# Layer 1's output projections in seven block products between the feed-forward halves

## The chip, the cores and the metric

The kernel runs on one core of a Trainium2 chip. A core has TensorE (PE: matmuls, with the loads of their stationary operand shown apart as PEld), VectorE (DVE), ScalarE (ACT), GpSimd (POOL) and SyncE (SP), each with an instruction queue of its own, and 16 engines for transfers (DMA). Matmuls read SBUF and write PSUM[...]; all other data lie in SBUF or in DRAM. The metric is the device time of one execution in microseconds; the median of several is taken.

## The reference

Two layers, each an attention block and a gated feed-forward block, on 2048 tokens of 1024 features. Both layers use the same weights.

```python
x = x + _A_ref(_layernorm(x), wqkv, wo)
x = x + _B_ref(_layernorm(x), w1, w3, w2)     # twice over
# _A_ref: qkv = x @ wqkv; 32 heads of 32; each token attends to 8 tokens, 2 apart, itself and back;
#         softmax over the 8; o = weighted sum of v; return o @ wo          (wo: 1024 x 1024)
# _B_ref: h = silu(x @ w1) * (x @ w3); return h @ w2                        (3584 wide)
```

The change concerns `o @ wo` of the second layer, which the kernel calls layer 1.

## The kernel before

Tokens go in chunks of 512 (`CH`), four to a layer. A unit is one chunk of one layer; `units` has eight, 0 to 3 of layer 0 and 4 to 7 of layer 1. Unit u runs the feed-forward block of its chunk (`b_stage`, L1276); while it does, the attention of a later chunk goes on in the background, and after it the query, key and value products of unit u + 3 are made (`q_part`, L837), for u from 1 to 4.

*The feed-forward block.* From unit 2 on (`TU`) it is computed by Strassen's scheme in Winograd's form: a product of two matrices is cut into 2 x 2 blocks and made in seven block products, P1 to P7, in place of eight, with sums of blocks made before and after. `products` (L1143) does one of the two parts into which the 3584 hidden features are split, 2048 and 1536 (`fsplits`; called halves below). `pipeline` (L1052) makes the hidden features in groups of four tiles of w1 or w3; `second` (L1226) then multiplies by w2's half, with `W(name, j)` (L1179) for one block product and one of two tiles of 128 tokens. Bank A holds P1, is copied to bank B by ScalarE, and both go on: P2 is added to B, P6 and then P7 and P4 to A, P5 and P3 in D. The copies of A and D that VectorE adds (`s5`, `su`) are ScalarE's. So P2 or P6 waits for the copy after P1, P7 for the copy after P6, and P3 and P4 for VectorE's sums. `output` adds a finished bank to the residual `x_sb`.

*The sums of the weights.* The block sums of w1, w3 and w2 are made in units 0 and 1 (`weight_sums`, `sums_of_w2`): ScalarE scales four blocks into fp16, VectorE makes three differences and a sum, GpSimd's queue stores the seven blocks to DRAM (`t_d`, `t2_d`), and later they are loaded as any weight. The scale is a power of two from the sum of squares (`weight_size`, `total_scale` at L995). For w2 and w1/w3 there are two such buffers; `stored[a]` is the time at which the planner takes a buffer's last store to have landed, 7.0 us after the last difference.

*The attention.* `score_steps` (L583) and `value_steps` (L664) yield VectorE instructions for halves of 256 tokens: products of q and k with sums over each head's lanes in a tree (into `psm`, L593), a matmul that gathers the heads, a softmax, a copy of the weights to all lanes by GpSimd's queue (`At`), products with v and the second tree (into `oT`, in two buffers).

*The output projection.* `o_tile` (L772) does 128 tokens: eight matmuls into each of two 512-column banks, each added to `x_sb` by VectorE. For both layers, it is called from `between` (L814), which runs after each feed-forward group and takes a tile whose `oT` is ready. When a chunk's four tiles are done, its layer norm is queued.

*What sets the order.* The order is written by a planner inside the kernel, when it is built: each engine has a planned time (`now`), each background step a cost and a time at which it is ready. `background` (L135) puts VectorE steps ahead of the next fixed one where they fit; `act_background` (L363) does so for ScalarE's lists, up to `gate` (2.2 us) ahead of TensorE; `finish_sums` and `force` empty a list at once. `load_weight` (L715) requests the weight tiles in the order of the list `seq` on SP's queue, into six buffers, one as each is released.

Of the kernel before, what the change touches and what calls it, by code (L numbers as in the profile page):

```python
# [17 lines left out]
def kernel(  # L18
# [13 lines left out]
    nc = tc.nc  # L32
# [178 lines left out]
    NG = NF // FG  # L211
    ones = const.tile([P, P], FP32, name="ones")
# [8 lines left out]
    peak = const.tile([P, 3], FP32, name="peak")  # L221
    hsum = const.tile([P, HTN // 2, HT], FP16, name="hsum")
    h16 = hT[:].bitcast(FP16)
    t2_d = [dram.tile([P, 7, (b - a) // 2, 512], FP16, name=f"t2_d{i}") for i, (a, b) in enumerate(fsplits)]
    t_d = [[dram.tile([P, 14, KT // 2, P], FP16, name=f"t_d{m}_{g}") for g in range(NG)] for m in range(2)]
    qkv_d = [[dram.tile([P, KT, S], BF16, name=f"qkv_d{l}_{i}") for i in range(3)] for l in range(2)]
# [74 lines left out]
    adds, acts, makes, reads, parts, sizes = [], [], [], [], [], []  # L301
# [61 lines left out]
    def act_background():  # L363
        for queue in (acts, sizes, parts, reads):
            while True:
                s = head(queue)
                if s is None or max(now["act"], s[1]) + s[0] > now["pe"] + gate[0]:
                    break
                take_act(queue)
# [213 lines left out]
    def score_steps():  # L583

        V = nc.vector
        for g, (l, h) in enumerate(halves):
# [6 lines left out]
            psm = wk.tile([P, W, 2, TCH], BF16, name="psm")  # L593
# [6 lines left out]
            parts_ = 2 if l == 0 else 1  # L600
# [6 lines left out]
            def gather_heads(t, parts_=parts_):  # L607
                at["L"] = L = side_tile([P, W, BLK], FP32, name="L", tag="sd")
                for i in range(parts_):
                    for a in range(4):  # L610
                        nc.tensor.matmul(L[32 * a:32 * (a + 1), :, :], lhsT=gather[:],  # L611
                                         rhs=psm[:, :, i, a * BLK:(a + 1) * BLK], start=i == 0, stop=i == parts_ - 1,
                                         skip_group_check=True)
                at["t"] = pe(1.5 * parts_, t) + 0.2
# [38 lines left out]
            yield 0.56, 0.0, lambda: V.reciprocal(rs[:], sm_[:])  # L653
            yield 0.68, 0.0, lambda: V.tensor_tensor(An[:], E[:], rs[:].unsqueeze(1).to_broadcast([P, W, BLK]),
# [9 lines left out]
    def value_steps():  # L664

        V = nc.vector
        for g, (l, h) in enumerate(halves):
            while (l, h) not in At_at or (g >= 2 and o_todo.get(halves[g - 2], 1)):
                yield "blocked"
            load_v(l, h)  # L670
            while (l, h) not in vs:
                yield "blocked"
                load_v(l, h)
            At = Ats[l, h]
            vT, ready = vs[l, h]
            oT = wk.tile([P, KT, TCH], BF16, name="oT", bufs=2)
            oTs[l, h] = oT

            def mul_v(t, tm):
                base = vT[:, t, HALO:HALO + TCH]  # L680
                win = bass.AP(vT.tensor, base.offset, [list(base.ap[0]), [-DIL, W], [BLK, 4], [1, BLK]])
                V.tensor_tensor(tm.rearrange("p w (a e) -> p w a e", a=4), At[:].rearrange("p a w e -> p w a e"), win, op=ALU.mult)  # L682

            yield 0.0, max(ready + 2.0, At_at[l, h]), lambda: None
            yield from tree(KT, tree_bufs[1], mul_v, lambda t: oT[:, t, :], False)
            oT_at[l, h] = now["dve"]
            o_todo[l, h] = 2
            av_done.add((l, h))
            if g + 1 < len(halves):
                load_v(*halves[g + 1])  # L690
# [5 lines left out]
    for u in range(len(units)):  # L696
        for f0, f1 in fsplits:
# [9 lines left out]
            if u >= TU:  # L707
                seq += [("t2", fsplits.index((f0, f1)), b, nq) for b in range(7)]
            else:
                seq += [("w2", g0, nq, hh) for hh in range(2) for g0 in (f0, f0 + nq)]  # L710
# [4 lines left out]
    def load_weight(pieces=1):  # L715
# [11 lines left out]
        elif kind == "t2":  # L727
            w = wp.tile([P, 8, 512], FP16, name="t2", tag="w")
            nc.sync.dma_start(w[:, 0:rest[0], :], t2_d[i][:, n])
            at = dma(128 * rest[0], now["pe"])  # L730
        elif kind in ("early", "late"):
# [105 lines left out]
    def q_part(l, c, which, ws, then=()):  # L837
# [8 lines left out]
        for t0 in range(0, KT, SG):  # L846
# [19 lines left out]
            if l == 0:  # L866
                stored[:] = landed, landed
# [65 lines left out]
    pending, stored, made, held = [0] * 2, [0.0] * 2, set(), []  # L933
# [36 lines left out]
    def measure2(i, n, at):  # L970

        w = hT[:, 0:n, :]
        for a, b in ((0, n // 2), (n // 2, n)):
            def square():
                nc.scalar.activation(junk[:, 0:(b - a) * 512], w[:, a:b, :].rearrange("p k c -> p (k c)"),
                                     ACTF.Square, accum_out=size2[:, len(measured):len(measured) + 1])
                measured.append(i)
                if len(measured) == 16:
                    total_scale(size2, up2, down2, got2)
# [15 lines left out]
    def total_scale(sizes_, up, down, got):  # L995
# [3 lines left out]
        def scale_item(ps, r):  # L999
            def emit():  # L1000
                opened[0] -= 1
                nc.vector.tensor_reduce(total[:], ps[:], op=ALU.add, axis=AX.X)
                scale_of(total[:], up[:], down[:])
# [3 lines left out]
        def add_up(t):  # L1007
            ps = side_tile([P, n], FP32, name="size", tag="sd")
            opened[0] += 1
            nc.tensor.matmul(ps[:], lhsT=ones[:], rhs=sizes_[:], start=True, stop=True)  # L1010
# [5 lines left out]
    got2 = {}  # L1016

    def sums_of_w2(i, f, ws, loaded):

        while "at" not in got2 or all(pending):  # L1020
            yield "blocked"
# [30 lines left out]
    def pipeline(key, groups, consume, done, last, fill=None):  # L1052
# [68 lines left out]
        for i in range(n + 1):  # L1121
# [19 lines left out]
            done(i)  # L1141

    def products(u, f0, f1, hold):  # L1143
# [118 lines left out]
        def done(i):  # L1262
            if i and groups[i - 1]["m"] == 1:
                h_pieces(groups[i - 1]["f"] + FG)
            if i < len(groups):
                between(hold)
            q = u + 3
# [8 lines left out]
    def b_stage(u, hold):  # L1276
# [5 lines left out]
        for (f0, f1) in fsplits:  # L1282
            lastsplit = (f1 == fsplits[-1][1])
            if u >= TU:
                products(u, f0, f1, hold)
                continue
# [106 lines left out]
    for u, (l, c) in enumerate(units):  # L1393
        if u + 1 < len(units):
            l2, c2 = units[u + 1]
            o_queue += [(l2, c2 * TPC + j) for j in range(TPC)]
# [3 lines left out]
        if with_q:  # L1400
            for which in range(3):
                if which == 2:
                    between(False, True)
                q_part(*units[q], which, [weight("qkv"), weight("qkv")])
# [31 lines left out]
```

## Time and profile before

| | |
|---|---|
| median of 3 runs | 1531.34 us (1530.53 to 1531.69) |
| the profiled execution | 1530.2 us, its span 1528.5 us |
| TensorE busy | 1519.7 us, 9634 matmuls |
| VectorE busy | 1202.3 us |
| ScalarE busy | 884.7 us |
| output projections of both layers | 512 matmuls, 115.7 us |
| transfers | 439.56 MB, mean 288 GB/s |

Busy time is the time in which an engine has an instruction of the kernel; two that overlap count once. A row of the groups gives source line, engine, operation, what it writes and reads with shapes, the count, then busy time, the mean of one in ns, and after the bar the engine's idle time just before such instructions with what ended it. In the order of time a row begins with its start in us from the span's start and its length. By the order of time, unit 2's groups begin at 554.96 us, unit 3's at 740.93, unit 4's at 925.85, unit 5's at 1111.72, unit 6's at 1255.22 and unit 7's at 1396.92.

### The profile page before, as it was taken

The page shows a single profiled execution, that of the slowest core. Times are in us where ns is not written, and L with a number is a line of the kernel's source. Part 1 is how long each engine was busy: PE and PEld are TensorE (multiplying, and loading weights), DVE is VectorE, ACT ScalarE, POOL GpSimd, SP SyncE. Part 2 cuts the span into 40 slices and gives each one's busy share as a digit, 9 for nine tenths or more (in the row PEclk, how much of TensorE's full clock was granted, in tenths as well). Part 3 has the DMA queues.
Part 4 walks back from the last instruction along what each step waited for, and adds up shares of the span by engine and source line. Part 5 has one row for each costly group of instructions (what it writes and reads, how often), then busy time and mean ns, then how long its engine had stood idle before and what let it go on. Part 6 is the DMA issues. An engine that isn't in the chain of part 4 may idle for free.

```text
span 1528.5 us, 25134 instructions
## 1 busy us (share of the span) xinstructions
PE 1519.7 (99%) x9634; PEld 989.3 (65%) x9634; DVE 1202.3 (79%) x2126; ACT 884.7 (58%) x1388; POOL 160.0 (10%) x308
## 2 busy tenths in 40 slices
PE   9999999999999999999999999999999999999999
PEld 7666644444444577575786767766677768686865
DVE  4788998889889898979898959798678977535445
ACT  4785476567665357455465564755557446554643
POOL 1210102121211101002001020100111001000000
PEclk9999999999999999999999999999999999999999
DMA  9777969898997888979879888898969887878885
GB/s 336 192 224 215 260 218 334 279 300 283 309 307 257 278 317 293 350 271 294 264 268 356 323 259 282 271 335 304 322 224 331 337 315 266 306 273 336 317 293 204
DMA packets 261432, 439.56 MB, mean 288 GB/s; under 512 B 73856, under 2 KB 201088, under 8 KB 245056
## 3 DMA queue, kind: packets, MB, share of 16 engines
q1 hardware_dynamic: 248464, 390.90, 77.1%
q0 software_dynamic: 12704, 46.93, 8.6%
q8 instruction: 75, 1.23, 0.3%
q14 instruction: 45, 0.37, 0.1%
q10 hardware_dynamic: 144, 0.13, 0.0%
HBM read 345.90 MB, written 67.90 MB: 271 GB/s over the span
## 4 chain that ended last, share of the span: by engine, by line
PE 94%; ACT 3%; DVE 2%; issue 1%; DMA 0%; SPq 0%; ACTq 0%; DVEq 0%
PE st L1069 31%; PE ps L853 21%; PE w L1188 15%; PE po L788 7%; PE pg L1302 6%; PE acc L1333 6%; PE pu L1311 6%; PE pq L444 1%; ACT sg L1250 1%; PE L L611 0%; ACT L639 0%; DMA wqkv<-in_A_wqkv_dram 0%; DVE hT L1159 0%; DVE tree L597 0%; ACT L1250 0%
## 5 line engine op out<-in xcount | busy, mean ns | idle before, releaser
L853 PE MATMUL ps<-xnT,wqkv 128*128 128x512 f16 (+1 forms) x1472 | 320.5, 379 | 0.0
L1069 PEld LDWEIGHTS <-early 128*128 128x128 f16 x2688 | 262.6, 98 | 40.5 <-issue 3.5
L853 PEld LDWEIGHTS <-wqkv 128*128 128x128 bf16 x1472 | 210.7, 144 | 108.0 <-issue 2.2
L1188 PE MATMUL w<-t,hT 128*128 128x512 f16 x1008 | 225.9, 379 | 1.2 <-ACT big L1208 1.1
L1069 PEld LDWEIGHTS <-late 128*128 128x128 f16 x2016 | 197.2, 98 | 28.9 <-issue 1.1
L597 DVE TENSOR_TENSOR tree<-qT,kT 128x2048 bf16<-128x2048 bf16 x128 | 156.2, 1220 | 30.3 <-DMA kT<-qkv_d 14.5
L510 DVE TENSOR_TENSOR tree<-tree 128x1024 bf16<-128x1024 bf16 x256 | 174.8, 684 | 1.0
L1069 PE MATMUL st<-xnT,late 128*128 128x256 f16 x1344 | 174.2, 273 | 0.4 <-DVE big L1106 0.2
L1069 PE MATMUL st<-big,early 128*128 128x256 f16 x1344 | 172.2, 273 | 1.5 <-ACT st L1081 1.4
L1188 PEld LDWEIGHTS <-hT 128*128 128x128 f16 x1008 | 98.3, 98 | 113.7 <-issue 2.4
L1069 PE MATMUL st<-xnT,early 128*128 128x256 f16 x1344 | 165.8, 273 | 0.0
L682 DVE TENSOR_TENSOR tree<-At,vT 128x2048 bf16<-128x2048 bf16 x128 | 156.0, 1218 | 9.3 <-DMA At<-E 8.0
L1081 ACT COPY st<-st 128x512 f32<-128x512 f32 x84 | 48.3, 575 | 125.9 <-PE st L1069 125.2
L788 PE MATMUL po<-wo,oT 128*128 128x512 bf16 x512 | 115.7, 379 | 0.0
L1311 PE MATMUL pu<-xnT,w3t 128*128 128x512 f16 x448 | 105.8, 379 | 0.0
L1302 PE MATMUL pg<-xnT,w1t 128*128 128x512 f16 x448 | 105.8, 379 | 0.0
L857 ACT CAST hT<-ps 128x512 bf16<-128x512 f32 x96 | 55.6, 585 | 86.4 <-PE ps L853 83.0
L1333 PE MATMUL acc<-w2t,hT 128*128 128x512 bf16 x448 | 98.3, 379 | 0.0
L1094 DVE TENSOR_TENSOR st<-st,big 128x512 f32<-128x512 f32 x84 | 58.3, 695 | 45.4 <-ACT big L1090 45.2
L1250 ACT ACTIVATE sg<-st,down_scale 128x512 bf16<-128x512 f32 x126 | 86.7, 688 | 11.9 <-PE st L1069 11.6
L1069 PE MATMUL st<-big,late 128*128 128x256 f16 x672 | 87.1, 273 | 0.0
L788 PEld LDWEIGHTS <-oT 128*128 128x128 bf16 x512 | 50.1, 98 | 55.7
(167 smaller groups left out, 1920.3 us busy)
## 6 DMA issues: line engine op xcount, KB each, us to landing
early<-t_d SPq DMA_DIRECT2D x84, 1024.0 KB, 6.7
late<-t_d SPq DMA_DIRECT2D x84, 768.0 KB, 6.4
t<-t_d SPq DMA_DIRECT2D x42, 1024.0 KB, 7.6
t<-t_d SPq DMA_DIRECT2D x42, 768.0 KB, 5.2
wqkv<-in_A_wqkv_dram SPq DMA_DIRECT2D x28, 1024.0 KB, 7.5
w1t<-in_B_w_dram SPq DMA_DIRECT2D x14, 1024.0 KB, 7.8
w3t<-in_B_w_dram SPq DMA_DIRECT2D x14, 1024.0 KB, 11.3
t_d<-big POOLq DMA_DIRECT2D x28, 512.0 KB, 5.5
```

The costliest lines, as they stand in the source:

```text
L510: nc.vector.tensor_tensor(b, b, buf[:, 4:8, :], op=ALU.add)
L597: V.tensor_tensor(pr, qT[:], kT[:, :, k0:k0 + TCH], op=ALU.mult)
L682: V.tensor_tensor(tm.rearrange("p w (a e) -> p w a e", a=4), At[:].rearrange("p a w e -> p w a e"), win, op=ALU.mult)
L788: nc.tensor.matmul(ps[:], lhsT=oT[:, t, j * P:(j + 1) * P], rhs=wo[:, t, hh * 512:(hh + 1) * 512], start=(t == 0), stop=(t == KT - 1))
L853: nc.tensor.matmul(ps[:], lhsT=ws[kk // KH][:, kk % KH, t::KT], rhs=xnT[:, kk, :], start=(kk == 0), stop=(kk == KT - 1))
L1069: nc.tensor.matmul(out[:, a, :], lhsT=w[:, a, blk, k, :], rhs=rhs[:, k, :], start=start and a == 0 and k == 0, stop=k == KQ - 1, skip_grou ...
L1094: nc.vector.tensor_tensor(G["D"][:], G["D"][:], su, op=ALU.add)
L1188: nc.tensor.matmul(out[:], lhsT=lhs[:, k, j * P:(j + 1) * P], rhs=w[:, k, :], start=start and k == 0, stop=k == nq - 1, skip_group_check=True)
L1250: nc.scalar.activation(sg[:], src, ACTF.Silu, scale=inv)
L1302: nc.tensor.matmul(pg[:], lhsT=w1t[:, kk, fi * P:(fi + 1) * P], rhs=xnT[:, kk, :], start=(kk == 0), stop=(kk == KT - 1))
L1311: nc.tensor.matmul(pu[:], lhsT=w3t[:, kk, fi * P:(fi + 1) * P], rhs=xnT[:, kk, :], start=(kk == 0), stop=(kk == KT - 1))
L1333: nc.tensor.matmul(acc[:], lhsT=hT[:, f, j * P:(j + 1) * P], rhs=tiles[hh][f // nq][:, f % nq, :], start=(f == 0), stop=(f == f1 - f0 - 1))
```

## The change

Layer 1's output projections are made by the same scheme of seven products, as a stage of its own for a whole chunk (`o_products`), after the first half of units 3 to 6. Layer 0's keep `o_tile`. A chunk's two halves of 256 tokens are the rows of blocks, the two halves of wo's 1024 input features the other cut of the left side, and two column halves of 512 that of wo.

For that wo needs its block sums. Sums of squares of wo and of wqkv's value part, in 16 ScalarE instructions, give two powers of two. In unit 2 the sums are made in eight small blocks: four scaled copies on ScalarE, four VectorE instructions and one store by GpSimd's queue each, in one buffer, `spare`. It lies in the half of the score buffer (`psms`, now a fixed tile of the size of `psm`) that only layer 0's scores use. In unit 3, SP's queue loads four of the seven blocks over wo (`wo16`); the other three come for each chunk as two weight tiles ("to"). Layer 1's `oT` is fp16, and its softmax denominators take one of the scales; the outputs are scaled on their way into `x_sb`.

```diff
+    psms = const.tile([P, 2 * W * TCH], BF16, name="psms")
+    spare = psms[:, W * TCH:W * TCH + 7 * TCH].bitcast(FP16).rearrange("p (b c) -> p b c", b=7)
+    wo16 = wo[:].rearrange("p k d -> p (k d)").bitcast(FP16).rearrange("p (b f c) -> p b f c", b=4, f=KT // 2)
...
-        for queue in (acts, sizes, parts, reads):
+        for queue in (acts, sizes, parts, reads, lazy):
...
+            if l == 1:
+                while "at" not in got_a[2]:
+                    yield "blocked"
+                yield 0.12, got_a[2]["at"], lambda: V.tensor_scalar(rs[:], rs[:], up_a[:, 1:2], None, op0=ALU.mult)
...
+                if f0 == 0 and u + 1 < len(units) and units[u + 1][0] == 1:
+                    seq += [("to", 4, 2), ("to", 6, 1)]
...
+        elif kind == "to":
+            w = wp.tile([P, 8, 512], FP16, name="to", tag="w")
+            nc.sync.dma_start(w[:, 0:4 * n, :], to_d[:, i:i + n].rearrange("p b f c -> p (b f) c"))
...
+    def sizes_of(m, w, i0, at):
+        for k in range(w.shape[1]):
+            yield 1.10, at, lambda: nc.scalar.activation(junk[:, 0:D], w[:, k, :], ACTF.Square,
+                                                         accum_out=size_a[:, m, i0 + k:i0 + k + 1])
+        if i0 + w.shape[1] == KT:
+            total_scale(size_a[:, m, :], up_a[:, m:m + 1], down_a[:, m:m + 1], got_a[m])
...
+    def sums_of_wo(at):
+        KQ = KT // 2
+        while (0, NCH * R - 1) not in At_at:
+            yield "blocked"
+        for f, q in ((f, q) for f in range(KQ) for q in range(2)):
+            while pending[2]:
+                yield "blocked"
+            pending[2] += 1
+            for j, (fh, hh) in ((0, (0, 0)), (2, (0, 1)), (1, (1, 0)), (5, (1, 1))):
+                c0 = hh * 512 + q * TCH
+                yield 0.37, max(at, stored[2]), lambda: nc.scalar.activation(
+                    spare[:, j], wo[:, KQ * fh + f, c0:c0 + TCH], ACTF.Copy, scale=up_a[:, 0:1])
+            makes.append([sums_of_wo_block(f, q, now["act"] + 0.1), None])
+        made.add("wo")
+
+    def sums_of_wo_block(f, q, r):
+        for out, x, y in ((4, 5, 2), (2, 2, 0), (3, 4, 0), (6, 1, 3)):
+            yield 0.28, r, lambda: nc.vector.tensor_tensor(
+                spare[:, out], spare[:, x], spare[:, y], op=ALU.add if (x, y) == (4, 0) else ALU.subtract)
+        pending[2] -= 1
+        nc.gpsimd.dma_start(to_d[:, :, f, q * TCH:(q + 1) * TCH], spare)
+        stored[2] = now["dve"] + 7.0
...
+    def o_products(c, hold):
...
+        def h_sum(name, out, x, y, op, r):
+            background(r)
+            nc.vector.tensor_tensor(out, x, y, op=op)
+            at[name] = dve(0.61, r) + 0.1
...
+        def run(name, j, out, start, r=0.0):
+            for k in range(KQ):
+                nc.tensor.matmul(out[:], lhsT=left[name][:, k, j * P:(j + 1) * P], rhs=right[name][:, k, :],
+                                 start=start and k == 0, stop=k == KQ - 1, skip_group_check=True)
+            return pe(KQ, max(r, at.get(name, 0.0)))
...
+        for j in range(2):
+            g = G[j]
+            g["A"] = bank("oA")
+            g["1"] = r = run("P1", j, g["A"], True)
+            g["B"] = bank("oB")
+            nc.scalar.copy(g["B"][:], g["A"][:])
+            g["tB"] = act(0.5, r)
...
+        for j in range(2):
+            g = G[j]
+            r = run("P6", j, g["A"], False, g["tB"])
+            nc.scalar.copy(su[j], g["A"][:])
+            g["tU"] = t = act(0.5, r)
+            background(t + 0.8)
+            nc.vector.tensor_tensor(g["D"][:], g["D"][:], su[j], op=ALU.add)
+            g["tD"] = dve(0.68, max(t, g["t5"])) + 0.1
+        w = weight("to")
+        right["P7"], right["P3"] = w[:, 0:KQ], w[:, KQ:KT]
+        for j in range(2):
+            g = G[j]
+            r = run("P7", j, g["A"], False, g["tU"])
+            background(r + 0.8)
+            nc.vector.tensor_tensor(s22[j], g["A"][:], s5[j], op=ALU.add)
+            g["tC"] = dve(0.68, r) + 0.1
+            output(2 + j, 1, s22[j], g["tC"])
...
+            if (u, f0, i) == (2, 0, 2):
+                finish_sums(lambda: "at" in got_a[0] and "at" in got_a[1])
+                scale_o()
+                reads.append([sums_of_wo(now["act"]), None])
+            if (u, f0, i) == (3, 0, 5):
+                finish_sums(lambda: "wo" in made)
+                force(makes, lambda: not pending[2])
+                nc.sync.dma_start(wo16, to_d[:, 0:4])
+                dma(2048)
...
                 products(u, f0, f1, hold)
+                if f0 == 0 and u + 1 < len(units) and units[u + 1][0] == 1:
+                    o_products(units[u + 1][1], hold)
...
-            o_queue += [(l2, c2 * TPC + j) for j in range(TPC)]
+            if l2 == 0:
+                o_queue += [(l2, c2 * TPC + j) for j in range(TPC)]
...
-                q_part(*units[q], which, [weight("qkv"), weight("qkv")])
+                ws = [weight("qkv"), weight("qkv")]
+                if u == 1 and which == 0:
+                    lazy.append([sizes_of(0, wo, 0, 0.0), None])
+                if u == 1 and which == 2:
+                    lazy.extend([sizes_of(1, ws[i], KH * i, w_at[used[0] - 2 + i]), None] for i in range(2))
+                q_part(*units[q], which, ws)
+                while which == 2 and head(lazy) is not None:
+                    take_act(lazy)
                 release(2)
```

The stage runs P1, P2, P5, P6, P7, P3 and P4 in that order, each for two tiles of 128 tokens, with bank A, B and D and the copies as in `second`, but with a second buffer for the copy of A (`su`).

## The prediction

> **What bounds the kernel now.** I read the page first, then TensorE's waits, then busy time in stretches of layer 1, and last the order of time at the places where the change puts work.
>
> ```profile
> PE 1519.7 (99%) x9634; PEld 989.3 (65%) x9634; DVE 1202.3 (79%) x2126; ACT 884.7 (58%) x1388; POOL 160.0 (10%) x308
> PEclk9999999999999999999999999999999999999999
> ...
> PE 94%; ACT 3%; DVE 2%; issue 1%; DMA 0%; SPq 0%; ACTq 0%; DVEq 0%
> ...
> L788 PE MATMUL po<-wo,oT 128*128 128x512 bf16 x512 | 115.7, 379 | 0.0
> ```
>
> The clock is full throughout and the chain that ended last is 94% matmuls: time falls where matmuls are removed and nothing makes TensorE wait. The last line is the work that the change touches: 512 output-projection matmuls, half of them layer 1's, with no idle time before any. They start 0.216 us apart (sixteen start between 744.43 and 747.88 us); 379 ns is the latency of one.
>
> Busy time by stretch: unit 2 (555 to 741 us), two second halves in unit 3 and 4 that hold feed-forward groups without an output projection in them, and the first half of unit 4, which has four. Columns are length, then busy us of PE, PEld, DVE, ACT, POOL, then clock, DMA share and GB/s.
>
> ```profile
> 555.00:741.00 186.00, 185.23 (x1254) 129.70 (x1253) 163.87 (x282) 110.90 (x176) 23.22 (x40) 1.00 0.89 303
> 829.00:863.00 34.00, 34.00 (x314) 30.46 (x313) 32.90 (x59) 23.23 (x37) 0.00 (x0) 1.00 0.91 325
> 1015.00:1049.00 34.00, 34.00 (x314) 30.48 (x313) 33.18 (x63) 22.56 (x37) 0.00 (x0) 1.00 0.90 308
> 926.00:988.00 62.00, 61.28 (x497) 47.97 (x495) 49.68 (x87) 38.60 (x63) 3.55 (x10) 1.00 0.76 269
> ```
>
> Two things count. VectorE is 88% busy in unit 2 and 97% in the second halves, so work added to it there is late. And groups run without a gap when no output projection stands between them, so taking the projections out of the first halves costs nothing by itself. TensorE's waits between 741 and 1397 us (units 3 to 6) sum to 2.2 us:
>
> ```profile
> PE st L1069 <- ACT st L1081: 1.0, 2, 0.6
> PE w L1188 <- ACT big L1208: 0.8, 2, 0.5
> ```
>
> All are of one kind: a ScalarE copy of a partial sum is late and the next product on that bank waits for it.
>
> [...]
>
> **The change part by part.**
>
> *Products.* Layer 1 has four chunks of 64 matmuls (4 token tiles x 2 column halves x 8). Seven products of 2 token tiles x 4 matmuls are 56. Saved: 4 x 8 x 0.216 = 6.9 us. The two new sums of squares on TensorE are two passes each, whose starts are 29 and 111 ns apart in the trace: 0.14 us each, 0.3 us.
>
> *The squares.* Sixteen squares of 128x1024 come into unit 1's query/key/value part, one behind each evacuation. A like ACT instruction (L318) lasts 1.06 us and its read of the sum 0.20, overlapping to 1.05 us from start to start; with the evacuation's 0.48 that is 1.53 in the 1.73 us in which TensorE makes one output. It fits, but the order shows that the last square stands behind the last evacuation and ahead of the first copy of unit 2. Before, that place looks so:
>
> ```profile
> 554.96 1.04 PE L1069 MATMUL st<-xnT,early 128*128 128x256 f16 x8
> ...
> 555.21 0.59 ACT L857 CAST hT<-ps 128x512 bf16<-128x512 f32 x1 [1.15 <-PE ps L853]
> ...
> 555.83 1.91 PE L1069 MATMUL st<-big,early 128*128 128x256 f16 x16
> ...
> 556.09 0.57 ACT L1081 COPY st<-st 128x512 f32<-128x512 f32 x1 [0.29 <-PE st L1069]
> ```
>
> The copy at 556.09 must end before P6, eight matmuls into the third line, at 556.70. With the square it starts at 555.21 + 0.48 + 1.05 = 556.74 and ends at 557.32: TensorE loses 0.7 us, once.
>
> *The block sums in unit 2.* Eight blocks of four scaled copies (128x256; half of L927's 0.71 us) and four VectorE differences (0.28 us each by the 128x256 row of L514): 12 us on ScalarE, which has 75 idle in the stretch, and 9 us on VectorE, which has 22. So VectorE goes to 93% and its sums and outputs slip. There is one buffer: the next block's first copy waits on ScalarE's queue for the store to land. The planner reckons with 7.0 us after the last difference. The nearest stores, also of 896 rows:
>
> ```profile
> t_d<-big POOLq DMA_DIRECT2D x14, 896.0 KB, 6.4
> ```
>
> and the copies that wait for such a store behind them already stand idle in the trace of before (the waits of L1026):
>
> ```profile
>   DMA t_d<-big: 34.9, 11
> ```
>
> A block is half as many bytes, so it should land in about 6 us from an issue some 0.5 us after the last difference; some will be later than 7. Behind the waiting copy stand the bank copies that P6 and P7 need, with about 1.6 us to spare (three products of 0.87 us, less 0.4 until the result is seen and a copy of 0.58). Cost: nothing if landings are in time, 1.4 us for each of 7 refills if they come 10 us after the last difference. I take 0.8 for landings and 1.5 for VectorE's slip: 2.3 us. The stores stand on POOL's queue among the attention copies; POOL is busy 23 us of the 186, so I take nothing for that.
>
> *The new stage.* One product of a token tile is 4 x 0.216 = 0.86 us. P1's result must be copied to a second bank before P2: last start 0.65, seen 0.42 later (at the border in unit 3, where P4's output starts 0.20 after the next product does, 828.80 against 828.60), copy 0.58, pick-up 0.05, sum 1.70 against the 1.73 after which P2 comes. P6 to P7 is the same. Both hold by 0.03 us, if nothing stands ahead of the copy on ScalarE; the order shows nothing. VectorE has 4 sums of 1024 (0.61 us from start to start, of L1159), 8 outputs (0.67, L1173) and 4 adds (0.60, L1211): 10.2 us in TensorE's 12.1. But the order puts 8, 5, 8 and 0 attention instructions among them, 3.6, 2.6, 3.6 and 0 us. So in three of the four stages VectorE ends 2 to 3 us late. What is late next: P4 of the second tile waits for its sum (about 0.1 to 0.6 us), and the next half's P5 takes a bank that an output frees with three outputs (2.0 us) behind it, so about when P5 comes. I take 0.3 us a stage, 1.2 in all; bounds 0 and 2 us a stage. Before, the same border (828.60, P5 at 829.47) has no wait.
>
> *Loads.* 1.5 MB for each chunk, 2 MB once on SP's queue in unit 3, and 3.7 MB of stores. The once-load waits for the stores: the order puts the last of them at the start of unit 2's query/key/value part, which takes 41.7 us (699.0 to 740.7), and five groups of 6.1 us follow before the load, so they have landed. At 300 GB/s it delays the weight tiles behind it on SP's queue by 7 us. In a second half of before a tile is asked for about 12 us before its use and lands in 6.7, a cover of 5 us: taken at 0, up to 2 us if that fails. In the new stage no weight is asked for, so the queue catches up.
>
> *Other.* Waits that move in the first halves, +0.5 us. The scaling of a 128x64 row, the two-byte type of oT and the fixed score buffer change no duration that I can see.
>
> Sum: -6.9 + 0.3 + 0.7 + 2.3 + 1.2 + 0.5 = -1.9 us. The profiled execution took 1530.2 us, its span 1528.5; so 1528.3 and 1526.6. The median of the runs is 1.1 above that execution: 1529.4 us.
>
> **The rivals.**
> *All waits are hidden.* The pipelines without projections have none in 34 us, and ScalarE has room. Then only the sums of squares and the late square remain: 1531.3 - 6.9 + 1.0 = 1525.4. Against it: VectorE at 97%.
> *The store decides, slower.* Without its 0.8 us the gain is 2.7. If every block lands 9.6 us after its last difference, ScalarE's queue is held 2.6 us beyond plan, less 1.6 to spare: 1 us for each of 7 refills, 7 in all: 1531.3 - 2.7 + 7 = 1535.6. It turns the sign from 0.4 us a refill, a landing 9.0 us after the last difference. For it: the 34.9 us above, a median of 6.4 and a plan of 7.0. Against: half the bytes.
> *VectorE in the new stage.* If it is 2 us late in each of four stages, 8 in place of 1.2: 1536. Against: three outputs lie behind the one that frees the bank, and the last stage has no attention in it.
> *The change only moves the bound.* 11.7 MB more at a DMA share of 0.9 would take 39 us if all of it stood in the way; the chain has DMA at 0%, so a few late tiles: 1532 to 1534.
>
> **How the numbers follow.** Forecast 0.52, in its own range of 1527.3 to 1531.5; all hidden 0.16; the store 0.12; VectorE 0.10; loads 0.10. 0.2%, about what a measurement of this kernel can tell from no change, is 3.06 us: faster is under 1528.28, slower over 1534.40. Faster: all of the second and a quarter of the first, 0.28. Slower: the store and VectorE in most cases, 0.18. The rest, 0.54, is no difference. The range leaves out a tenth at each end: 1525.2 to 1535.2.
>
> **What would show it.** Layer 1's projections with 224 matmuls at 0.216 us and four stages of 12.1 to 12.7 us; a wait of about 0.7 us on a ScalarE copy at the start of unit 2; unit 2 longer by 2 to 4 us and units 3 to 6 shorter by 5 to 6 together. Wrong if ScalarE's waits for the store exceed some us a refill, if a stage takes over 13.5 us, or if TensorE waits for a weight tile.

## The result, and the profile after

The changed kernel took 1537.41 us, the median of 4 runs (1536.69 to 1539.18), beside 1530.93 us (1530.49 to 1531.69) for the kernel before on the same chip: a ratio of 1.0044, 95% interval 1.0026 to 1.0061. It is 6.5 us slower; a time of 1529.4 us, 1.9 less, was forecast. Two of the changed kernel's four runs, 1538.13 and 1539.18 us, show a mean clock of 0.999, while the other two at 1.000 lie 5.8 us above the kernel before. The profiled execution took 1536.69 us, its span 1535.0.

The page of the changed kernel: its engines, TensorE's clock, and the chain of work that ended last.

```profile
PE 1516.7 (99%) x9606; PEld 986.7 (64%) x9606; DVE 1232.4 (80%) x2210; ACT 924.5 (60%) x1476; POOL 157.5 (10%) x316
...
PEclk9999999999999999999999999999999999999999
...
PE 39%; DVE 11%; ACT 4%; issue 2%; DMA 1%; POOL 0%; ACTq 0%; DVEq 0%; POOLq 0%
```

TensorE has less to do than before (1519.7 us) and the clock is full in this execution, so the time is in waits. The chain can't be set beside that of before, in which TensorE had 94%: its shares add up to 57%, as it is followed back only to 662.4 us, where it comes to a store. In the part that it covers VectorE, ScalarE and a transfer have a share. Such shares are not costs, but they name where to look.

The groups by shape show the work that was exchanged (layer 0's tiles first, then the new stage; after the bar, the idle time before such a matmul):

```profile
L805 PE MATMUL po<-wo,oT 128*128 128x512 bf16 x256 | 57.9, 379 | 0.2 <-DVE x_sb L810 0.2
L1231 PE MATMUL oA<-to,oT 128*128 128x512 f16 x64 | 15.4, 379 | 1.3 <-DVE big L1275 1.3
L1231 PE MATMUL oA<-wo,oT 128*128 128x512 f16 x64 | 15.1, 379 | 0.0
L1231 PE MATMUL oD<-wo,hsum 128*128 128x512 f16 x32 | 7.6, 379 | 0.0
L1231 PE MATMUL oD<-to,oT 128*128 128x512 f16 x32 | 7.6, 379 | 0.0
L1231 PE MATMUL oB<-wo,oT 128*128 128x512 f16 x32 | 7.6, 379 | 0.0
```

256 of layer 1's matmuls have become 224 of the same length: 32 x 0.216 = 6.9 us are gone. The saving is real, and 13 us of other time came.

Busy time by unit, 2 to 5 (the columns as in the prediction):

```profile
555.60:747.60 192.00, 186.37 (x1255) 129.63 (x1253) 170.02 (x317) 122.04 (x211) 24.43 (x44) 1.00 0.92 308
747.60:933.90 186.30, 183.19 (x1240) 128.90 (x1237) 153.56 (x259) 114.03 (x181) 17.02 (x40) 1.00 0.94 310
933.90:1117.30 183.40, 182.92 (x1237) 128.84 (x1236) 155.41 (x266) 111.70 (x179) 14.75 (x36) 1.00 0.95 315
1117.30:1262.40 145.10, 142.09 (x1046) 101.43 (x1045) 135.66 (x234) 84.07 (x136) 8.76 (x18) 1.00 0.90 310
```

Before, these units took 185.9, 184.9, 185.9 and 143.5 us. Unit 2, where the block sums are made, is 6.1 us longer. Unit 4 is 2.5 us shorter, near the 1.7 us of the eight matmuls that each of units 3 to 6 lost; units 3 and 5, which lost as many, are longer. From the start of unit 3 to that of unit 7 it is 655.9 us in place of 656.0. So there are two things to explain: unit 2's 6.1 us, and that units 3 to 6 give back all of what they save. What TensorE waited for:

```profile
PE st L1126 <- ACT big L1147: 3.8, 4, 3.0
PE st L1126 <- ACT sg L1405: 2.3, 2, 1.1
PE st L1126 <- DVE st L1151: 1.4, 1, 1.4
PE oA L1231 <- DVE big L1275: 1.3, 2, 0.7
PE w L1343 <- ACT big L1363: 1.3, 3, 0.7
```

Each line is a waiting matmul, what it waited for, the sum, the count and the longest. One wait of 3.0 us for the copy of A (`su`, L1147) is the largest. In order of time, all engines, it looks so:

```profile
634.10 0.28 DVE L1069 TENSOR_TENSOR psms<-psms 128x256 f16<-128x256 f16 x1
...
634.93 0.96 POOL L1072 DMA_DIRECT2D to_d<-psms  x1 [11.95 <-DVE psms L1069]
...
639.34 0.57 ACT L1138 COPY st<-st 128x512 f32<-128x512 f32 x1 [5.74 <-PE st L1126]
...
640.89 1.91 PE L1126 MATMUL st<-xnT,early 128*128 128x256 f16 x16
...
643.84 0.51 ACT L1061 ACTIVATE psms<-wo,up_a 128x256 f16<-128x256 bf16 x1 [3.92 <-DVE tree L519]
644.25 0.58 ACT L1143 ACTIVATE big<-st 128x512 f32<-128x512 f32 x1
644.73 0.50 ACT L1061 ACTIVATE psms<-wo,up_a 128x256 f16<-128x256 bf16 x1
645.13 0.57 ACT L1147 COPY big<-st 128x512 f32<-128x512 f32 x1
...
645.75 0.49 PE L1126 MATMUL st<-xnT,late 128*128 128x256 f16 x3 [2.95 <-ACT big L1147]
```

And the one store of that stretch, from the view of transfers (KB, us from issue to landing):

```profile
to_d<-psms POOLq DMA_DIRECT2D x1, 448.0 KB, 8.5
```

The block's last difference ends at 634.38, GpSimd issues the store at 634.93, and it lands 8.5 us later at 643.5: 9.1 us after the difference, where the planner wrote 7.0. The next block's first scaled copy (L1061) is at the head of ScalarE's queue from 639.9 on and can't write the one buffer until then; ScalarE stands idle for 3.92 us. (The line names a VectorE instruction, L519, as what ended that. It isn't connected with the copy; the landing is what the copy needs.) Behind it stand the copies of D and A (L1143, L1147), whose products were made by 640.9, and P7 on TensorE, due at 642.6, waits for the second.

To compare whole kernels I add, from unit 2 on, the time by which each matmul starts later after the one before than their usual distance (0.108 us for 256 columns, 0.216 for 512), where that is over 0.15 us and the trace shows a releaser:

| us of lateness on TensorE | before | after |
|---|---|---|
| start of unit 2 (to 612 us) | 0 | 1.4 |
| rest of unit 2 and the border to unit 3 | 1.3 | 5.7 |
| behind an exponential and its tables in unit 3 | 0 | 2.6 |
| the new stages and the product after each | 0 | 1.9 |
| all else | 3.6 | 5.7 |
| sum | 4.9 | 17.3 |

12.4 more, less the 6.9 saved, plus the 0.6 by which unit 2 begins later, is 6.1; the spans differ by 6.5.

### The profile page after: what moved, and what is told of

It reads as the page before. It is cut to its first block, busy times and chain, and to the rows that moved or that the text cites. A ratio compares the mean times of both kernels' runs of the same rounds, so it can differ in the third digit from the quotient of the medians.

```text
span 1535.0 us, 25327 instructions
## 1 busy us (share of the span) xinstructions
PE 1516.7 (99%) x9606; PEld 986.7 (64%) x9606; DVE 1232.4 (80%) x2210; ACT 924.5 (60%) x1476; POOL 157.5 (10%) x316
## 4 chain that ended last, share of the span: by engine, by line
PE 39%; DVE 11%; ACT 4%; issue 2%; DMA 1%; POOL 0%; ACTq 0%; DVEq 0%; POOLq 0%
PE st L1126 20%; PE w L1343 10%; PE ps L870 7%; DVE tree L605 1%; DVE tree L517 1%; ACT sg L1405 1%; DVE x_sb L1328 1%; PE oA L1231 1%; DVE hT L1314 1%; DVE tree L693 1%; DVE hT L1414 1%; DVE tree L519 1%; ACT xn L325 1%; PE oD L1231 0%; DMA to_d<-psms 0%
## 5 line engine op out<-in xcount | busy, mean ns | idle before, releaser
L605 DVE TENSOR_TENSOR tree<-qT,kT 128x2048 bf16<-128x2048 bf16 x128 | 156.2, 1221 | 19.5 <-DMA qT<-qkv_d 14.4
L693 DVE TENSOR_TENSOR tree<-At,vT 128x2048 bf16<-128x2048 bf16 x128 | 156.1, 1220 | 13.6 <-DMA At<-E 12.4
L1151 DVE TENSOR_TENSOR st<-st,big 128x512 f32<-128x512 f32 x84 | 58.5, 696 | 58.8 <-ACT big L1147 58.3
L1405 ACT ACTIVATE sg<-st,down_scale 128x512 bf16<-128x512 f32 x126 | 86.6, 687 | 10.3 <-PE st L1126 9.9
L519 DVE TENSOR_TENSOR tree<-tree 128x512 bf16<-128x512 bf16 x192 | 80.3, 418 | 0.0
L1503 PEld LDWEIGHTS <-hT 128*128 128x128 bf16 x448 | 43.7, 98 | 53.2 <-issue 0.8
## 6 DMA issues: line engine op xcount, KB each, us to landing
w3t<-in_B_w_dram SPq DMA_DIRECT2D x14, 1024.0 KB, 12.1
```

Source lines behind the costliest of these rows:

```text
L519: nc.vector.tensor_tensor(b[:, 0:2, :], b[:, 0:2, :], b[:, 2:4, :], op=ALU.add)
L605: V.tensor_tensor(pr, qT[:], kT[:, :, k0:k0 + TCH], op=ALU.mult)
L1151: nc.vector.tensor_tensor(G["D"][:], G["D"][:], su, op=ALU.add)
L1405: nc.scalar.activation(sg[:], src, ACTF.Silu, scale=inv)
L1503: nc.tensor.matmul(acc[:], lhsT=hT[:, f, j * P:(j + 1) * P], rhs=tiles[hh][f // nq][:, f % nq, :], start=(f == 0), stop=(f == f1 - f0 - 1))
```

## The experiments

Two theories stood against each other at first. *The store*: its landing beyond the plan makes the loss. *Full engines*: VectorE and ScalarE are too full for the block sums and the stage, and the store's wait is only where it shows. "The later plan" is the kernel that is told of sixth.

**The blocks stored from elsewhere.** The sums are made, but the store reads another DRAM tensor.

```diff
-        nc.gpsimd.dma_start(to_d[:, :, f, q * TCH:(q + 1) * TCH], spare)
+        nc.gpsimd.dma_start(to_d[:, :, f, q * TCH:(q + 1) * TCH], t2_d[0][:, :, f, q * TCH:(q + 1) * TCH])
```

> Changed kernel, same order on every engine, but the eight stores of unit 2 take their bytes from another DRAM tensor, so no scaled copy waits for a store to land. Left out: wo's real sums (layer 1's projections use w2's blocks). Theory landing (ScalarE stands at the head of its queue until a store has landed, and a bank copy behind it is late): the 3.1 us wait at 645.7 us and most of those at 671 to 690 go, unit 2 is 3.5 to 4.5 us shorter, time about 1533.3. Theory amount of work (ScalarE's and VectorE's added instructions make unit 2 longer, whatever they wait for): within 0.7 us of the changed kernel, 1537.4.

1535.66 us, ratio 1.0028 (1.0017 to 1.0040). Unit 2 fell to 187.3 us, but the run doesn't tell the theories apart, since the edit moved something else: with no block to wait for, the eight stores were issued from 276.9 to 298.3 us, in unit 0, and near them TensorE lost 2.77 us and then ran at a lower clock, 0.90 from 290 to 306 us (order of time, TensorE):

```profile
298.03 1.89 PE L1481 MATMUL pu<-xnT,w3t 128*128 128x512 f16 x8
302.69 5.30 PE L805 MATMUL po<-wo,oT 128*128 128x512 bf16 x16 [2.77 <-DVE x_sb L810]
```

Sixteen matmuls that take 3.6 us take 5.3. Unit 2 begins 4.3 us later than in the changed kernel; from there to the last matmul's start it takes 968.7 us against 975.6. That is the size of the loss, but a comparison of a part.

**No block sums at all**; the stage loads block sums of w2 in their place, so that the projections have wrong weights.

```diff
...
-                reads.append([sums_of_wo(now["act"]), None])
+                made.add("wo")
...
-                nc.sync.dma_start(wo16, to_d[:, 0:4])
+                nc.sync.dma_start(wo16, t2_d[0][:, 0:4, 0:4])
```

> Changed kernel without the eight blocks of copies, differences and stores; the stage loads w2's block sums in wo's place (left out: wo's sums, so layer 1's projections are of other weights). Theory landing and theory amount of work alike: unit 2 falls to 0.7 to 1.5 us above the kernel before (the late square stays), time 1530.5 to 1532. Theory stage (the loss comes from the new stage and from what it shifts in units 3 to 6): time stays above 1535.

1534.82 us, 1.0027 (1.0018 to 1.0036): a miss, between the two times expected. Unit 2 is 187.3 us and unit 3 184.0, but unit 5 is 148.2. There an exponential fell into a gate group. In order of time, ScalarE and TensorE:

```profile
1222.57 1.28 ACT L646 ACT_TABLE_LOAD   x1
1222.69 1.04 PE L1126 MATMUL st<-xnT,late 128*128 128x256 f16 x8
1223.86 0.60 ACT L646 ACTIVATE E<-L 128x512 bf16<-128x512 f32 x1
1224.47 1.28 ACT L1405 ACT_TABLE_LOAD   x1
1225.77 0.69 ACT L1405 ACTIVATE sg<-st,down_scale 128x512 bf16<-128x512 f32 x1
...
1226.51 1.86 PE L1126 MATMUL st<-big,early 128*128 128x256 f16 x8 [2.79 <-ACT sg L1405]
```

The exponential and the silu need different tables; both loads and the exponential, 3.2 us, stand before a silu that holds a bank. And again the clock is lower afterwards, 0.80 from 1226.6 to 1234.0 us: the eight matmuls of the last line take 1.86 us, those of the second 1.04. The four new stages take 1.6 us more in all than in the changed kernel (12.6, 13.9, 13.1 and 12.1 us). Taking work out moved the plan into other waits.

**The block sums alone**, layer 1's projections as before (`o_tile`); the kernel before with the squares, the scaled copies, the differences and their stores.

> Kernel before with the squares, the scales and the eight blocks of unit 2 of the changed kernel, their result unused; layer 1's projections by single tiles as before. Theory landing or amount of work: about 6 us above the kernel before (0.3 for sums of squares, 0.6 for the late square, 5 for the blocks), 1537. Theory stage: 1 us above, 1532.

1543.90 us, 1.0082 (1.0067 to 1.0097): 13 us for the sums and squares without the stage, twice the 6 that were expected of them. So the loss is there without any stage. What the stage itself is worth can't be read from the 6.5 us between this kernel and the changed one, since the plan is another: TensorE's largest other losses are 1.49 us at 850.23, 1.84 at 1027.27 and 1.36 at 1124.83. The copies wait for the store about as in the changed kernel, where five wait for 8.1 us with the 3.92 above (the waits of L1055, the copy's line here):

```profile
  DMA to_d<-psms: 8.8, 6
```

**No attention in the stage**: its calls of `background` go, so that nothing stands between its sums.

```diff
-            background(r)
             nc.vector.tensor_tensor(out, x, y, op=op)
...
-            background(r + 0.8)
             nc.vector.tensor_tensor(s22[j], g["A"][:], s5[j], op=ALU.add)
```

> Changed kernel in which no attention instruction is put among VectorE's work of the new stage. If VectorE's attention work makes P4 of the second tile late in stages one and three (waits of 0.9 and 0.8 us): both waits go, 1.5 to 1.9 us faster than the changed kernel, 1535.7, unless the attention that is put off is missed later. If they come from VectorE's own chain: no change, 1537.4.

1537.34 us, 1.0035 (1.0022 to 1.0049), by the median level with the changed kernel. But both waits in the stage are gone, and all four stages take 12.1 us. In the profiled execution (1537.83 us, mean clock 0.999) the eight matmuls behind the store's wait in unit 2 take 1.86 us in place of 1.03 (last section), which hides a gain: from the start of unit 3 to the last matmul's it takes 782.5 us, the changed kernel 783.5. So of the 1.5 to 1.9 us expected about 1 came, by one execution of each kernel, and a part went where the attention went (waits of 0.9 us at 1247 and 0.7 at 1252). Some of what VectorE is spared in one place it owes in the next.

**The store from a buffer of its own.** The last difference goes into a small double buffer, and the store reads that, seven times over (as many bytes, but not the blocks, so that the projections have wrong weights). The next block's copies then wait for no store, and the order of the instructions is the same on every engine.

```diff
+    last = const.tile([P, 2, TCH], FP16, name="last")
...
-                spare[:, out], spare[:, x], spare[:, y], op=ALU.add if (x, y) == (4, 0) else ALU.subtract)
+                spare[:, out] if out < 6 else last[:, q], spare[:, x], spare[:, y], op=ALU.add if (x, y) == (4, 0) else ALU.subtract)
...
-        nc.gpsimd.dma_start(to_d[:, :, f, q * TCH:(q + 1) * TCH], spare)
+        nc.gpsimd.dma_start(to_d[:, :, f, q * TCH:(q + 1) * TCH], last[:, q].unsqueeze(1).to_broadcast([P, 7, TCH]))
```

> Changed kernel, same order on every engine; each block's last difference goes to a small buffer of its own, of which there are two, and the store sends that buffer seven times. So no scaled copy waits for a store, while the stores keep their time, size and queue. Left out: six of wo's seven sums (each is sent as the last one). Theory landing: unit 2 from 192.1 us (555.6 to 747.6) to 187 to 188, and 5 to 7 us less in all: 1530.5 to 1532. Theory amount of work: unit 2 stays above 191 us, time about 1537.

1530.48 us, 0.9997 (0.9988 to 1.0006). The same place in order of time:

```profile
633.52 0.96 POOL L1073 DMA_DIRECT2D to_d<-last  x1 [11.70 <-DVE last L1070]
...
638.91 0.57 ACT L1139 COPY st<-st 128x512 f32<-128x512 f32 x1 [5.39 <-PE st L1127]
639.39 0.51 ACT L1062 ACTIVATE psms<-wo,up_a 128x256 f16<-128x256 bf16 x1
639.81 0.58 ACT L1144 ACTIVATE big<-st 128x512 f32<-128x512 f32 x1
640.28 0.50 ACT L1062 ACTIVATE psms<-wo,up_a 128x256 f16<-128x256 bf16 x1
640.68 0.58 ACT L1148 COPY big<-st 128x512 f32<-128x512 f32 x1
```

This store still takes 8.1 us (view of transfers), and nobody waits: the copy of A starts 0.2 us after its product's matmuls (640.46) and not 4.2 after. The wait of 1.4 us at the start of unit 5 (L1151) is gone too, so it doesn't come without the store's wait. One cause is 6.9 us by the medians, or 6.1 by the spans of the two profiled executions, which both have the full clock.

**A later plan.** The planner reckons with 11.0 us until a block's store has landed.

```diff
-        stored[2] = now["dve"] + 7.0
+        stored[2] = now["dve"] + 11.0
```

> Changed kernel in which the planner takes a block's store to have landed 11.0 us after its last difference in place of 7.0; everything that follows is planned anew. Theory landing: no copy waits over 0.5 us for a store, unit 2 falls to 187 to 189 us, time 1531 to 1534 as the new order has it. Theory amount of work: unit 2 stays above 191 us.

1530.70 us, 0.9999 (0.9991 to 1.0008). No copy waits for a store now. So the loss needs no other buffer to cure it; the plan had a number too small. But the kernel is only level with the one before: 6.9 us of matmuls are gone, and units 3 to 6 take 656.1 us in place of 656.0. By the same sum as above its lateness is 12.2 us: 1.4 at the start of unit 2, 1.6 in the rest of it and at the border, 2.6 behind exponentials, 1.9 in the stages, 4.7 elsewhere.

**No changes of table, in the changed kernel and in the one before.** Squares stand in for the softmax's exponentials. In the changed kernel's trace all 29 loads of a table stand at an exponential (14), a silu (14) or the square root at the start (1), none at a square.

```diff
-                    nc.scalar.activation(E[:], L[:], ACTF.Exp, scale=scale)
+                    nc.scalar.activation(E[:], L[:], ACTF.Square, scale=scale)
```

> Changed kernel, same order, with squares in place of the softmax's exponentials (so the softmax is not computed): ScalarE loads no function table after the first. Theory exponentials (the change moved softmax steps into feed-forward groups, where two table loads of 1.3 us hold a bank): the waits of 1.3 us at 760 and 848 go, and the gap to the kernel before that is treated in the same way shrinks from 6.5 to 4 us or less. Theory landing alone: the gap stays at 6 us.

> Kernel before, same order, with squares in place of the softmax's exponentials (so the softmax is not computed). Its waits of 0.6, 1.2 and 0.6 us at 675, 983 and 1158 come with table loads too: 2 us faster than the kernel before, 1529. If table loads cost nothing there: 1530.9.

1531.73 us, 1.0002 (0.9994 to 1.0011), and 1527.58 us, 0.9975 (0.9964 to 0.9985). The two waits of L1405 in unit 3 went. So did the one at the start of unit 5 (L1151, from 1.4 us to 0.03), though the store's wait stays with 2.8 us: that after-effect takes both. The tables cost 5.7 us in the changed kernel, and 3.4 in the one before, which hardly shows them: there they were behind its late copies of A to B (L1081). I took this at first for a second cause of 2.3 us.

**Both: the later plan without changes of table.**

> The changed kernel with a small block's store planned at 11.0 us in place of 7.0, and every exponential made a square (the softmax is then not a softmax; all other work and the order of it stay). This joins the two edits that were tried apart. If the store's landing and ScalarE's changes of table are the two things that took the 6.9 us back, what is left of the gain shows once both are gone: 1530.7 of the later plan alone less some 3.4 to 5.7 us that the tables cost in the two kernels, so 1525 to 1527, under the 1527.6 of the kernel before without tables. If the moved exponentials matter little once nothing waits for a store, the time is level with the kernel before without tables or above it, 1527.5 to 1528.5.

1526.69 us, 0.9974 (0.9964 to 0.9985). The number is the one expected, but the reading falls: it can't be told from the kernel before without tables (0.9975). With the store's wait gone the tables cost 4.0 us, near the 3.4 of the kernel before; most of the 2.3 us came only together with the store. A new wait came as well: 2.3 us for VectorE's tree at 743.26 us, the border to unit 3, where the later plan alone has 0.9.

**An exponential behind the last silu of a gate group**, in the changed kernel with the later plan, and in the kernel before.

```diff
-                run_later()
+                if "m" not in G:
+                    run_later()
...
                 consume(G, 2, G["A"][:], r)
+                if G.get("m") == 0:
+                    run_later()
```

> The later plan again, with the right exponential, but an exponential that falls into a feed-forward pipeline is issued behind the last silu of a gate group and no longer between an up group's copies or a gate group's sums: the next silu is then a whole group of products away. Both changes of table then lie where no silu of the same group waits for them. If it was the two changes and the exponential together, 3.2 us ahead of one silu, that held a bank of PSUM, the two waits of 1.3 us of unit 3 go, and the time is 1527 to 1529.5. If the exponentials, up to 25 us later, make the softmax late for the stages of the output projections, waits there grow and the time is 1532 or more.

> The kernel before with the same place for the exponential: it tells whether a gain of that place belongs to the change or to any kernel of this plan. The kernel before has fewer exponentials inside the feed-forward pipelines' gate groups, and its tables cost 3.4 us in all: 1529 to 1530.9 (a gain of 0 to 2 us). If the late softmax decides: 1532 or more.

1530.06 us, 0.9997 (0.9989 to 1.0006), and 1531.56 us, 1.0006 (0.9998 to 1.0014): both outside what was expected, and neither to be told from the kernel before. The waits of 1.3 us did go, and others came, the largest in the second halves' copies:

```profile
PE w L1346 <- ACT big L1366: 3.1, 5, 0.8
```

**Layer 1's attention products on half of their columns**, with the later plan and in the kernel before; the two product lines of the trees (L605 and L693 in the changed kernel), the first of them:

```diff
-                V.tensor_tensor(pr, qT[:], kT[:, :, k0:k0 + TCH], op=ALU.mult)
+                V.tensor_tensor(*[z[:, :, 0:TCH // (1 + l)] for z in (pr, qT, kT[:, :, k0:k0 + TCH])], op=ALU.mult)
```

> The changed kernel with the later plan for the small blocks' stores, and layer 1's attention products made on half of their columns (128 instructions of 128x1024 in place of 128x2048, some 0.6 us less each, 75 us of VectorE's time in units 2 to 6 and about 6% of those units; the plan and its costs stay, the other half of the columns is stale, so layer 1's attention is not the reference's). If it is VectorE, too full to be in time, that takes the 6.9 us back in units 3 to 6 even where nothing waits for a store, most of its waits go there (10 us against 3.6 in the kernel before): 1523 to 1526.5. If the waits come from ScalarE's order and its changes of table, which VectorE's load doesn't touch, they stay: 1529 to 1531.

> The kernel before with the same halved products. It has few waits that VectorE ends, so with VectorE as the cause it falls by 0 to 2.5 us, to 1528.5 to 1531, and the changed kernel with the later plan comes out 2 us or more under it. If VectorE is not the cause, the two stay level within 1 us.

1526.26 us, 0.9970 (0.9957 to 0.9982), and 1529.00 us, 0.9990 (0.9983 to 0.9996). With some 60 us less of busy time on VectorE (1172.4 us in place of 1232.1 with the later plan) the changed kernel gains 4.4 us and the one before 1.6 (groups by shape, the halved products: 685 and 684 ns in place of 1220). The change is then ahead by 2.7 us (1526.08 to 1526.44 us against 1528.77 to 1530.36 on one chip). TensorE's waits of the changed kernel with the halved products:

```profile
PE st L1126 <- ACT sg L1405: 2.3, 2, 1.1
PE pw L200 <- DVE tree L195: 1.2, 1, 1.2
PE w L1343 <- ACT big L1363: 1.0, 2, 0.7
PE st L1126 <- ACT st L1138: 0.9, 2, 0.5
```

The waits in the stage (L1275) have fallen below what the view lists, and the two late stages take 12.25 and 12.31 us where they took 12.95 and 12.90; the wait for VectorE's tree at the border to unit 3 is gone too, and those for ScalarE's silus and the second halves' copies stay. VectorE's load is 2.8 us of what the change gives back, shown by the difference of the two kernels.

## Why the prediction was wrong

By its own terms, in its order:

- *Products, -6.9.* As forecast: 224 matmuls at 0.216 us.
- *Squares, +0.3 and +0.7.* The wait at the start of unit 2 came where it was placed, on the copy of A to B at 557.96 us, and is 0.63 us. Unit 2 begins 0.6 us later. Right, but two smaller waits follow in the same half (0.57 and 0.18).
- *Block sums, +2.3, of which 0.8 for landings.* **This step failed.** With the store's wait gone the time falls by 6.7 to 6.9 us by the medians and by 5.8 to 6.1 by the spans at full clock (the later plan; the store apart), so the landings were worth more than seven times their price. Two readings in it were wrong. The first was "half as many bytes, so it should land in about 6 us": the issue-to-landing times are 5.5, 7.9 and 8.7 us (least, median, most) for the 448 KB blocks, the median more than the 6.4 us of 896 KB that the prediction had quoted. The spread, too, could be read in the kernel before, where the prediction took the median. From issue to landing its 14 stores of 896 KB (L1035) and the 28 of 512 KB on the same queue (L943) took:

```profile
DMA to landing us min/median/max: 4.3/6.4/9.6
DMA to landing us min/median/max: 3.1/5.5/9.0
```

Little over half of the bytes bring the median down by 0.9 us, the longest by 0.6. The second reading that was wrong was the shape of the price. It spread 0.8 us over seven refills with 1.6 us to spare each. What was measured is five refills for which ScalarE waits, 0.4 to 3.9 us, and one of them cost TensorE 3.1 us, because there two bank copies were queued behind the waiting one. The smaller waits that went with the store's were under 0.6 us each, and one of 1.4 us stood 480 us later.

- *The new stage, +1.2.* 12.96, 12.09, 12.91 and 12.11 us: late in two of four by about 0.8, 1.7 in all, and 0.25 on the product after the first. The mechanism, VectorE's attention between the sums, is shown by the kernel without it, where all four take 12.1 us, and by the halved products. A mis-sized term, by 0.7.
- *Loads, 0.* Right: no wait for a tile of wo's sums or for a feed-forward weight.
- *Other, +0.5.* Short. Even with the later plan the waits of units 3 to 6 sum to 10.2 us in place of 3.6, so 6.6 more, where the stage and this term had 1.7. The prediction took "groups run without a gap when no output projection stands between them" to mean that what is taken out of the first halves is saved. The matmuls between the groups were also time in which VectorE and ScalarE caught up: with the later plan VectorE has 536.7 us of work in units 3 to 6, before it had 510.8, and TensorE has 7 us less to cover it with. For VectorE the halved products bear that out; for ScalarE it is argued.

The sum without any landing would have been -2.7; with the later plan the span says +0.7 and the medians -0.2. So the loss came from the store, and that the change gains nothing once it is mended comes from the other waits: VectorE's load for 2.8 us of it, the late square for 0.6. The rest, some 3 us of waits for ScalarE's copies and silus in changed places, is read from the trace and not taken apart by a run.

Of the rivals, *the store decides* had the right mechanism and place. That its 7 us for the store come near the 5.8 to 6.9 measured is luck: it gave 1 us to each of seven refills, and one made half of the sum. Its threshold, a landing 9.0 us after the last difference, fits by luck too: the block followed above landed after 9.1, but of the seven with a refill behind them only one more took over 9.0, and the others 6.0 to 8.9. Its time, 1535.6, was short, as it had the rest of the forecast in it. *All waits are hidden* is nowhere near, not even with the store mended. *VectorE in the new stage* has a part, after the store. *The bound moves to the loads* has nothing for it.

## What to carry to other kernels

When a planned landing time guards a single buffer, its error is paid by what stands behind the waiting copy on that engine's queue (here, at one refill, 3.92 us of ScalarE and 2.95 of TensorE): take the longest landing that the trace shows for such a store (here 9.6 us before the change), not the median or a share by bytes, and find the refill with the most behind it. A product that is removed need not save its time: here 6.9 us of matmuls went, and with the later plan 7.3 us of lateness came (12.2 in place of 4.9). VectorE was 82 to 93% busy in units 2 to 5; in such a stretch, count what it has to do in the time that remains. Undo a suspected wait with the order of the instructions kept; three of these edits that changed the order put new waits in other places.

## What was not expected of the hardware

In five profiled executions a wait of TensorE of 2.3 to 2.9 us was followed by a lower clock. In the kernel without block sums it was so after 2.79 us (busy time in two stretches, before and after that wait ended; the clock is the third figure from the end):

```profile
1219.00:1226.60 7.60, 4.82 (x45) 4.15 (x43) 7.57 (x13) 7.54 (x11) 0.00 (x0) 0.97 1.15 286
1226.60:1234.00 7.40, 7.40 (x56) 6.00 (x56) 5.10 (x11) 5.41 (x10) 0.00 (x0) 0.80 0.44 146
```

The eight matmuls behind that wait take 1.86 us and the eight after them 1.69, in place of 1.04. It was so after 2.77 us in the kernel with its stores from elsewhere (302.69: sixteen matmuls in 5.30 us in place of 3.6), after 2.91 without attention in the stage (646.00) and after 2.77 in the changed kernel without changes of table (647.19), both with a mean clock of 0.999 over the execution, and after 2.32 with the later plan and no changes of table (743.26; 0.998). It was not so after 2.95 us in the changed kernel, whose clock is 1.00 from 640 to 660 us. One and the same product, P7 behind the late copy of A in unit 2, ran both ways, in the changed kernel and without attention in the stage:

```profile
645.75 1.03 PE L1126 MATMUL st<-xnT,late 128*128 128x256 f16 x8 [2.95 <-ACT big L1147]
646.00 1.86 PE L1126 MATMUL st<-xnT,late 128*128 128x256 f16 x8 [2.91 <-ACT big L1147]
```

What the lower clock cost is an estimate from such stretches: it is short of full by 0.03 over 7.60 us and 0.20 over 7.40 in the kernel without block sums, 1.7 us in all, and by 0.10 over 16 us with the stores from elsewhere, 1.6 us. So a wait of this length cost some 1.6 to 1.7 us more there than where the clock stayed full. What decides whether the clock falls was not shown. And a change of ScalarE's table took 1.28 us each time, so one exponential among silus takes 3.2 us of its queue, five times its own 0.60.
